# Turning one batch's queries and keys with full-width transposes, their rows sorted in the copies

## The chip, the cores and the metric

One core of one Trainium2 chip. The metric is device time in microseconds (us) of the whole kernel. A timed run lasts about 1.9 us longer than the span from first to last instruction that a profile shows. Some runs show a mean granted clock (the share of TensorE's full clock that it was given) of 0.985 to 0.995 in place of 1.000 and are longer; the ratios below count them.

## The reference

Causal attention with 16 extra "beacon" keys and values per head, then a gated feed-forward block on the result.

```python
B, H, S, Nb, D = 8, 8, 576, 16, 64
k_all = concat([beacon_k, k], axis=2); v_all = concat([beacon_v, v], axis=2)
a = softmax(where(causal, -1e9, q @ k_all.T / sqrt(D)))
x = (a @ v_all) as (4608 tokens, 512)
out = (gelu(x @ w_gate) * (x @ w_val)) @ w_out        # 512 -> 1536 -> 512
```

Before the scores of a batch can be computed, queries and keys must stand with D on the partitions: they must be turned. Batches 2 to 7 are turned by DMA. Batches 0 and 1 are turned by TensorE; three of batch 1's four head pairs are turned inside the feed-forward part of the first chunk of tokens, and it is these three turns that change.

## The kernel before

Six tokens of one head lie in a row of the loaded tile (96 rows of 6 x 64). A turn transposes 64 columns at a time, so that the two heads of a pair land on the two halves of the partitions, in a bank pair of PSUM (the memory that TensorE writes to), out of the three-buffer pool that the gate and value products also use.

```python
def tr_part(b, m, w, dst):                    # m: head pair, w: 0 queries, 1 keys
    qk, kb = qk6[b]
    for r in range(6):
        for hi in range(2):
            tr(dst[64*hi : 64*hi+64, r*96 : (r+1)*96],
               qk[0:96, w, 2*m+hi, r*D : (r+1)*D])
    if w:
        tr(dst[:, S:SK], kb[:, 2*m : 2*m+2, :])      # the beacon: 16 rows, 128 columns

def transpose_pe(b, m, by_act=False):
    t_ps = psum_s.tile([P, 2, 1024], BF16, name="t_ps", tag="s")
    for w in range(2):
        tr_part(b, m, w, t_ps[:, w, :])
    # token = 6*t + r: one sorting copy of 576 each
    # keys by VectorE, queries by ScalarE, beacon by VectorE          (cut)

for fi in range(F_TILES):                     # first chunk (b == 0), 12 gate/value pairs
    if fi >= 2:
        gate_val(b, fi, ...)                  # 8 matmuls, gelu on ScalarE, product on VectorE
    if b == 0 and fi in (6, 7, 9):
        transpose_pe(1, min(fi - 6, 2), by_act=True)
    ...                                       # (cut)
```

`psum_t` lies idle in most of the first chunk, as does `psum_o`. And GpSimd issues the loads in line with the causal masks of the attention, five of batch 2's query loads directly ahead of batch 1's first mask (`ahead(n)` issues the next n loads).

The softmax here doesn't subtract the row's maximum and nothing guards it: scores larger than these inputs give would overflow.

Of the kernel before, what the change touches and what calls it, by code (L numbers as in the profile page):

```python
# [7 lines left out]
P = 128  # L8
B, H, S, NB, D = 8, 8, 576, 16, 64
SK = S + NB  # L10
# [31 lines left out]
BF16 = mybir.dt.bfloat16  # L42
ACT = mybir.ActivationFunctionType
# [6 lines left out]
def kernel(  # L50
# [12 lines left out]
    nc = tc.nc  # L63
    keep = tc.keep_in_program_order
# [10 lines left out]
    psum_t = ctx.enter_context(tc.tile_pool(name="psum_t", bufs=1, space=bass.MemoryType.PSUM))  # L75
    psum_o = ctx.enter_context(tc.tile_pool(name="psum_o", bufs=1, space=bass.MemoryType.PSUM))
# [26 lines left out]
    qkT = qkT_sb.rearrange("p (m w c) -> p m w c", m=NPAIR, w=2)  # L103
# [9 lines left out]
    qk6 = {}  # L113
# [34 lines left out]
    def load_qk(b):  # L148
        for load in qk_loads(b):
            load()  # L150

    def load_v(b):
        for load in key_loads(v, beacon_v, v_ring[b % NRING][:, :, :, 0:D], b):
            load()
# [15 lines left out]
    def act(out_ap, in_ap, func, **kw):  # L170
        keep(nc.scalar.activation(out_ap, in_ap, func, **kw))  # L171


    def tr(out_ap, in_ap):
        n = in_ap.shape[0]
        keep(nc.tensor.transpose(out_ap, in_ap, ident[0:n, 0:n]))  # L176

    def tr_part(b, m, w, dst):
# [4 lines that stand above are left out]
                    dst[64 * hi : 64 * hi + 64, r * 96 : (r + 1) * 96],  # L183
                    qk[0:96, w, 2 * m + hi, r * D : (r + 1) * D],
                )
        if w:
            tr(dst[:, S:SK], kb[:, 2 * m : 2 * m + 2, :])
# [5 lines that stand above are left out]
        out_ap = qkT[:, m, :, NB:SK].rearrange("p w (t r) -> p w t r", r=6)  # L193
        in_ap = t_ps[:, 0:2, 0:S].rearrange("p w (r t) -> p w t r", r=6)
        keep(nc.vector.tensor_copy(out_ap[:, 1], in_ap[:, 1]))
        if by_act:
            act(out_ap[:, 0], in_ap[:, 0], ACT.Copy)
        else:
            keep(nc.vector.tensor_copy(out_ap[:, 0], in_ap[:, 0]))
        keep(nc.vector.tensor_copy(qkT[:, m, 1, 0:NB], t_ps[:, 1, S:SK]))  # L200

    def transpose_half(b, m, w, by_act=False):
        pool, tag = ((psum_o, "o"), (psum_t, "t"))[w]
        t_ps = pool.tile([P, 1024], BF16, name="t_ps", tag=tag)
        for _ in range(8 if by_act else 0):
            tr(t_ps[0:D, 640:768], idle[:, 0:D])
        tr_part(b, m, w, t_ps)
        out_ap = qkT[:, m, w, NB:SK].rearrange("p (t r) -> p t r", r=6)
        in_ap = t_ps[:, 0:S].rearrange("p (r t) -> p t r", r=6)
        if by_act:  # L210
            act(out_ap, in_ap, ACT.Copy)
        else:
            keep(nc.vector.tensor_copy(out_ap, in_ap))  # L213
        return t_ps
# [14 lines left out]
    def transpose_dma(b):  # L229
        for w, ring_w in ((0, q_ring), (1, k_ring)):  # L230
            keep(
                nc.sync.dma_start_transpose(
                    out=qkT_by_tile[:, w].rearrange("p j m c -> p (j m) c"),
                    in_=ring_w[b % NRING].rearrange("p j h d -> p (j h d)"),
                )
            )

    def scores(b, *parts):
        s_ps = psum_s.tile([P, 2, 512], FP32, name="s_ps", tag="s")
        c0 = 0  # L240
        for m, c in parts:
            score_mms(b, m, c, s_ps[:, :, c0 : c0 + CHUNK_W[c]])
            c0 += CHUNK_W[c]
        (m, c), n = parts[0], len(parts)
        o, w = CHUNK_OFF[c], CHUNK_W[c]
        act(
            exp_ring[:, m : m + n, :, o : o + w].rearrange("p g h c -> p h g c"),
            s_ps[:, :, 0 : n * w].rearrange("p h (g c) -> p h g c", g=n),
            ACT.Exp,
            scale=QK_SCALE,  # L250
        )
        if b:
            for m, c in parts:
                masks(b, m, c)
# [87 lines left out]
    def av(b, m):  # L342
        x = psum_s.tile([P, 2, 512], FP32, name="x_ps", tag="s")
        for hi in range(2):
            attend(b, m, hi, x[:, hi, :])
        normalize(b, m, x, 0, 2)

    def av_head(b, m, hi, pool, tag):
        x = pool.tile([P, 1, 512], FP32, name="x_ps", tag=tag)
        attend(b, m, hi, x[:, 0, :])  # L350
        normalize(b, m, x, hi, hi + 1)
# [10 lines left out]
    def turn_dma(b, m):  # L362
        y_sb, y_before = y_of[b * NPAIR + m], y_of.pop((b - 1) * NPAIR + m)
        keep(nc.vector.tensor_copy(y_sb[0:NB, 0, :, :], y_before[KROWS[4] - NB : KROWS[4], 4, :, :]))
        c0 = b * S - NB
        keep(
            nc.sync.dma_start_transpose(
                out=xT_sb[:, m, c0 : c0 + 5 * P].rearrange("p (j n) -> p j n", n=P),
                in_=y_sb.rearrange("p j e d -> p (j e d)"),
            )  # L370
        )
# [3 lines left out]
    def hold(b, m):  # L375
        x = xT_sb[:, m, b * S : (b + 1) * S]
        keep(nc.gpsimd.tensor_copy(hold_sb, x[:, 0 : S : S - 1]))  # L377
# [53 lines left out]
    def gate_val(ci, fi, split=False):  # L431
        gv_mms(ci, fi, *range(K_CHUNKS), split=split, last=True)
# [27 lines left out]
    def out_mms(ci, u0, u1):  # L460
        for u in range(u0, u1):
            ti, fi = divmod(u, F_TILES)
            if u == 0:
                o_of[ci] = [opool.tile([P, 4, D_MODEL], FP32, name="o_sb", tag="o_sb"), None]
            if fi == 0:
                o_of[ci][1] = out_ps(ti)
            out_mm(ci, ti, fi, o_of[ci][1])
            if fi == F_TILES - 1:
                out_store(ci, ti, o_of[ci][1])
                if ci >= N_CHUNKS - 2:  # L470
                    store(nc.sync)
# [35 lines left out]
    def ahead(n):  # L507
        for load in loads[:n]:
            load()
        del loads[:n]  # L510
# [52 lines left out]
    for b in range(B):  # L563
        u = [0]

        def o(n):
            out_mms(b - 1, u[0], u[0] + n)
            u[0] += n

        if b:  # L570
            keep(nc.scalar.preload_act_table_set(SET_EXP))
            o(3)
            scores(b, (0, 0))
            scores(b, (0, 2))
            scores(b, (0, 1))
            o(5)
            if b == 1:
                transpose_pe(1, 3)
            ahead(2)
            o(5)  # L580
            scores(b, (0, 3), (1, 3))
            scores(b, (1, 0))
            scores(b, (1, 2))
            ahead(2)
            o(5)
            av_head(b, 0, 0, psum_t, "t")
            o(1)
            scores(b, (1, 1))
            scores(b, (2, 0))
            scores(b, (2, 2))  # L590
            ahead(2)
            av_head(b, 0, 1, psum_t, "t")
            turn_dma(b, 0)
            o(7)
            scores(b, (2, 1))
            scores(b, (2, 3), (3, 3))
            scores(b, (3, 0))
            av_head(b, 1, 0, psum_o, "o")
            o(5)
            av_head(b, 1, 1, psum_o, "o")  # L600
            turn_dma(b, 1)
            scores(b, (3, 1))
            scores(b, (3, 2))
            av(b, 2)
            turn_dma(b, 2)
            o(6)
            av(b, 3)
            turn_dma(b, 3)
            o(11)
            keep(nc.scalar.preload_act_table_set(SET_GELU))  # L610
            for kk in range(K_CHUNKS):
                for fi in range(2):
                    gv_mms(b, fi, kk, last=kk == 3)
        for fi in range(F_TILES):
            if fi >= 2:
                gate_val(b, fi, fi == F_TILES - 1 and b < B - 1)
            if b == 0 and fi in (6, 7, 9):
                transpose_pe(1, min(fi - 6, 2), by_act=True)
            if fi == 0:
                if b and b + 1 < B:  # L620
                    hold(b, 3)
                    load_v(b + 1)
                if b and b + 2 < B:
                    load_qk(b + 2)
                if 2 <= b + 1 < B:
                    transpose_dma(b + 1)
                store(nc.sync)
# [40 lines left out]
```

## Time and profile before

| | before |
|---|---|
| time, median of 6 runs (366.03 in the three that the prediction had) | 365.96 us (365.76 to 366.04) |
| span in the profile | 364.4 us |
| TensorE's share of the chain that ended last | 94% |
| TensorE's time in one turn (from the single records) | 0.837 us, three times |
| between the first gate product and the first output product of chunk 0 | 24.05 us |

The page, the chain and the timeline of a turn are shown in the prediction. A chain line gives start, length and what ran. A timeline line gives start, length, engine and instruction, `xN` for N merged ones, and in brackets how long the engine was idle before it and what ended that.

### The profile page before, as it was taken

How to read it: one execution, taken by the hardware profiler on the slowest of the kernel's cores; microseconds unless marked ns; L12 is line 12 of the kernel's file. 1: busy time of each engine (PE TensorE's matmuls, PEld its weight loads, DVE VectorE, ACT ScalarE, POOL GpSimd, SP SyncE). 2: the span in 40 equal slices, each digit the busy share in tenths (PEclk: the TensorE clock that was granted, in tenths of full speed). 3: DMA queues.
4: the chain of work that ended last, by engine and by line, in shares of the span. 5: the costliest groups of instructions: out<-in, count | busy, mean ns of one | idle time of the engine just before them, and what ended most of it. 6: DMA issues, size and time to landing. Idle time of an engine off the chain costs nothing.

```text
span 364.4 us, 7627 instructions
## 1 busy us (share of the span) xinstructions
PE 354.3 (97%) x3127; PEld 184.6 (51%) x3170; DVE 155.4 (43%) x305; ACT 189.0 (52%) x243; POOL 161.2 (44%) x288
## 2 busy tenths in 40 slices
PE   7899999999999999999999999999999999999996
PEld 6664446444654456445644464446544564444443
DVE  4546545433454335343533354434444353333332
ACT  3973489136933594339723892379335953321210
POOL 8934388565537452954475554646330530000000
PEclk9999999999999999999999999999999999999999
DMA  7999999799069995999299927991697033000103
GB/s 103 175 203 204 197 124 91 125 187 186 20 121 126 199 87 65 171 216 64 57 146 208 126 35 120 178 197 24 108 142 132 17 64 114 0 0 31 58 34 112
DMA packets 160419, 41.57 MB, mean 114 GB/s; under 512 B 146944, under 2 KB 155904, under 8 KB 160384
## 3 DMA queue, kind: packets, MB, share of 16 engines
q0 software_dynamic: 104848, 19.11, 69.5%
q1 hardware_dynamic: 55536, 21.96, 29.3%
q8 instruction: 25, 0.41, 0.5%
q14 instruction: 10, 0.08, 0.1%
HBM read 38.27 MB, written 9.44 MB: 131 GB/s over the span
## 4 chain that ended last, share of the span: by engine, by line
PE 94%; issue 1%; DMA 1%; DVE 1%; POOL 1%; POOLq 0%; DVEq 0%
PE gv_ps L168 48%; PE o_ps L168 25%; PE x_ps L168 9%; PE s_ps L168 8%; PE v_ps L168 2%; PE g_ps L168 2%; DMA qk<-in_q_dram 1%; PE t_ps L176 1%; DVE qkT L213 1%; POOL qk L111 0%; PE y_ps L176 0%; DVE hT_sb L426 0%; POOL eye L480 0%; DVE o_sb L445 0%; DVE qkT L217 0%
## 5 line engine op out<-in xcount | busy, mean ns | idle before, releaser
L171 ACT ACTIVATE ge_sb<-gv_ps 128x512 bf16<-128x512 f32 x101 | 59.4, 597 | 142.8 <-PE gv_ps L168 140.6
L426 DVE TENSOR_TENSOR hT_sb<-gv_ps,ge_sb 128x512 bf16<-128x512 f32 x101 | 69.0, 691 | 113.5 <-ACT ge_sb L171 111.1
L168 PE MATMUL gv_ps<-xT_sb,wg_sb 128*128 128x512 bf16 x402 | 111.4, 379 | 0.5
L168 PE MATMUL gv_ps<-xT_sb,wv_sb 128*128 128x512 bf16 x388 | 107.9, 379 | 0.4
L171 ACT ACTIVATE expT<-s_ps 128x992 bf16<-128x992 f32 (+3 forms) x112 | 100.6, 974 | 6.5 <-PE s_ps L168 5.4
L168 PE MATMUL o_ps<-wo_sb,hT_sb 128*128 128x512 bf16 (+2 forms) x420 | 99.9, 373 | 2.0 <-issue 0.9
L298 POOL TENSOR_SCALAR_AFFINE_SELECT expT<-expT 128x256 bf16<-128x256 bf16 (+1 forms) x140 | 52.3, 390 | 52.9 <-ACT expT L171 51.8
L168 PEld LDWEIGHTS <-wv_sb 128*128 128x128 bf16 x432 | 42.3, 98 | 50.6
L168 PEld LDWEIGHTS <-wg_sb 128*128 128x128 bf16 x432 | 42.0, 98 | 50.0
L168 PEld LDWEIGHTS <-hT_sb 128*128 128x128 bf16 x444 | 39.9, 98 | 41.7 <-issue 1.7
L168 PEld LDWEIGHTS <-expT 128*128 128x128 bf16 (+1 forms) x960 | 33.6, 97 | 9.8 <-DVE y_sb L334 2.9
L445 DVE COPY o_sb<-o_ps 128x512 f32<-128x512 f32 (+2 forms) x37 | 24.9, 672 | 31.2 <-PE o_ps L168 30.2
L168 PE MATMUL x_ps<-v_sb,expT 128*128 128x65 bf16 (+1 forms) x960 | 37.4, 193 | 0.0
L111 POOL DMA_DIRECT2D v_sb<-in_v_dram x40 | 33.6, 857 | 5.9 <-DMA wv_sb<-in_moe_w_val_dram 1.7
L168 PE MATMUL s_ps<-qkT 64*128 64x80 bf16 (+5 forms) x528 | 33.1, 250 | 2.3 <-DVE qkT L217 1.3
L111 POOL DMA_DIRECT2D k_sb<-in_k_dram x30 | 25.2, 842 | 14.7 <-DMA q_sb<-in_q_dram 11.3
L334 DVE TENSOR_TENSOR y_sb<-x_ps,r_sb 128x320 bf16<-128x320 f32 (+1 forms) x47 | 28.8, 612 | 1.6
L111 POOL DMA_DIRECT2D q_sb<-in_q_dram x30 | 25.3, 874 | 5.2 <-DMA wo_sb<-in_moe_w_out_dram 3.6
L332 DVE RECIPROCAL r_sb<-x_ps 128x5 f32<-128x5 f32 (+1 forms) x47 | 9.6, 204 | 42.3 <-PE x_ps L168 42.3
L168 PEld LDWEIGHTS <-qkT 64*128 64x128 bf16 x528 | 17.1, 95 | 17.8 <-issue 12.9
L377 POOL COPY hold_sb<-xT_sb 128x2 bf16<-128x2 bf16 x6 | 1.1, 186 | 31.1 <-DMA xT_sb<-y_sb 31.1
L111 POOL DMA_DIRECT2D k_sb<-in_beacon_k_dram x6 | 3.2, 534 | 13.4 <-DMA v_sb<-in_v_dram 13.4
(54 smaller groups left out, 123.3 us busy)
## 6 DMA issues: line engine op xcount, KB each, us to landing
out_dram<-o_sb SPq DMA_DIRECT2D x35, 256.0 KB, 7.0
v_sb<-in_v_dram POOLq DMA_DIRECT2D x24, 128.0 KB, 9.1
q_sb<-in_q_dram POOLq DMA_DIRECT2D x18, 128.0 KB, 11.8
k_sb<-in_k_dram POOLq DMA_DIRECT2D x18, 128.0 KB, 5.9
wo_sb<-in_moe_w_out_dram POOLq DMA_DIRECT2D x3, 512.0 KB, 14.4
wg_sb<-in_moe_w_gate_dram POOLq DMA_DIRECT2D x2, 512.0 KB, 11.4
wv_sb<-in_moe_w_val_dram POOLq DMA_DIRECT2D x2, 512.0 KB, 13.0
v_sb<-in_v_dram POOLq DMA_DIRECT2D x8, 112.0 KB, 5.4
```

Of the source, the lines that this page charges most:

```text
L111: keep(nc.gpsimd.dma_start(out=out_ap, in_=in_ap))
L168: keep(nc.tensor.matmul(out_ap, lhsT, rhs, start=start, stop=stop, **kw))
L171: keep(nc.scalar.activation(out_ap, in_ap, func, **kw))
L176: keep(nc.tensor.transpose(out_ap, in_ap, ident[0:n, 0:n]))
L213: keep(nc.vector.tensor_copy(out_ap, in_ap))
L298: nc.gpsimd.affine_select(out=d, in_=d, pattern=[[0, 2], [1, n]], compare_op=ALU.is_ge, fill=0.0, base=0, channel_multiplier=-1,)
L332: keep(nc.vector.reciprocal(r, x[:, :, :, D:DV]))
L334: nc.vector.tensor_tensor(out=y_of[i][:, :, h0:h1, :].rearrange("p j b d -> p b j d"), in0=x[:, :, :, 0:D], in1=r.to_broadcast([P, h1 - h0 ...
L377: keep(nc.gpsimd.tensor_copy(hold_sb, x[:, 0 : S : S - 1]))
L426: nc.vector.tensor_tensor(out=h_of[ci][:, fi, :], in0=gv_of.pop((ci, fi))[1], in1=ge_sb, op=ALU.mult)
L445: keep(nc.vector.tensor_copy(o_sb[:, ti, c0:c1], o_ps))
```

## The change

Two tokens of a head (128 columns) are transposed at once: 12 transposes and the beacon in place of 24 and the beacon. The half of the partitions now holds the even or odd token, no longer the head, so four copies per operand sort rows and tokens. The turns move to the idle banks and to pairs 4, 6 and 8.

```diff
+    def transpose_wide(b, m):
+        qk, kb = qk6[b]
+        for w in (1, 0):
+            pool, tag = ((psum_o, "o"), (psum_t, "t"))[w]
+            t_ps = pool.tile([P, 1024], BF16, name="t_ps", tag=tag)
+            for hi in range(2):
+                for r in range(3):
+                    c0 = (hi * 3 + r) * 96
+                    tr(t_ps[:, c0 : c0 + 96], qk[0:96, w, 2 * m + hi, r * P : (r + 1) * P])
+            if w:
+                tr(t_ps[:, S:SK], kb[:, 2 * m : 2 * m + 2, :])
+            for hi in range(2):
+                out_ap = qkT[64 * hi : 64 * hi + 64, m, w, NB:SK].rearrange("p (t r e) -> p t r e", r=3, e=2)
+                in_ap = t_ps[:, hi * 288 : (hi + 1) * 288].rearrange("p (r t) -> p t r", r=3)
+                for e in range(2):
+                    if w:
+                        keep(nc.vector.tensor_copy(out_ap[:, :, :, e], in_ap[64 * e : 64 * e + 64]))
+                    else:
+                        act(out_ap[:, :, :, e], in_ap[64 * e : 64 * e + 64], ACT.Copy)
+            if w:
+                keep(nc.vector.tensor_copy(qkT[:, m, 1, 0:NB], t_ps[:, S:SK]))
...
-            if b == 0 and fi in (6, 7, 9):
-                transpose_pe(1, min(fi - 6, 2), by_act=True)
+            if b == 0 and fi in (4, 6, 8):
+                transpose_wide(1, (fi - 4) // 2)
```

The intent: fewer TensorE instructions and fewer changes of the array's shape, paid with more work on two engines that have time.

## The prediction

> **What bounds the kernel now.** I read the page first, for the engine that carries the span, then the chain of work that ended last, then the chain in the stretch that the change touches (30 to 48 us, the feed-forward part of the first chunk, in which batch 1's queries and keys are turned), and last the timeline of one turn.
>
> ```profile
> span 364.4 us, 7627 instructions
> PE 354.3 (97%) x3127; PEld 184.6 (51%) x3170; DVE 155.4 (43%) x305; ACT 189.0 (52%) x243; POOL 161.2 (44%) x288
> ...
> PE 94%; issue 1%; DMA 1%; DVE 1%; POOL 1%; POOLq 0%; DVEq 0%
> ```
>
> TensorE carries 94% of the chain, VectorE and ScalarE are busy about half the time. So a change pays only through what it takes from TensorE's own time; work given to VectorE and ScalarE is free as long as no matmul comes to wait for it.
>
> The chain between 30 and 48 us (start, length, what):
>
> ```profile
> 32.23 3.18 PE gv_ps L168 x14
> 35.41 0.74 PE t_ps L176 x25
> 36.15 1.83 PE gv_ps L168 x8
> 37.98 0.74 PE t_ps L176 x25
> ...
> 39.10 3.19 PE gv_ps L168 x14
> 42.28 0.74 PE t_ps L176 x25
> 43.02 1.83 PE gv_ps L168 x8
> ```
>
> Each of the three turns is on the chain with 25 transposes, and gate and value matmuls follow directly. TensorE waits here for neither a PSUM buffer nor a copy. What there is to win is inside these three pieces. One of them, in the timeline (start, length, engine):
>
> ```profile
> 34.38 1.03 PE L168 MATMUL gv_ps<-xT_sb,wv_sb 128*128 128x512 bf16 x4
> 35.13 0.88 POOL L111 DMA_DIRECT2D v_sb<-in_v_dram  x1 [1.71 <-DMA wv_sb<-in_moe_w_val_dram]
> 35.34 0.57 PEld L176 LDWEIGHTS <-qk 96*64 96x64 bf16 x24 [0.42 <-issue]
> 35.34 0.70 PE L176 MATMUL t_ps<-eye,qk 96*64 96x96 bf16 x24
> ...
> 35.97 0.09 PEld L176 LDWEIGHTS <-kb 16*128 16x128 bf16 x1
> 35.98 0.18 PE L176 MATMUL t_ps<-eye,kb 16*128 16x16 bf16 x1
> 36.08 0.69 DVE L426 TENSOR_TENSOR hT_sb<-gv_ps,ge_sb 128x512 bf16<-128x512 f32 x1 [1.03 <-ACT ge_sb L171]
> 36.08 0.55 PEld L168 LDWEIGHTS <-wg_sb 128*128 128x128 bf16 x4
> 36.09 1.04 PE L168 MATMUL gv_ps<-xT_sb,wg_sb 128*128 128x512 bf16 x4
> 36.69 0.75 DVE L195 COPY qkT<-t_ps 128x576 bf16<-128x576 bf16 x1
> ...
> 37.47 0.65 ACT L171 ACTIVATE qkT<-t_ps 128x576 bf16<-128x576 bf16 x1 [1.42 <-DVE qkT L195]
> ```
>
> The single records of the trace resolve it: the last value matmul before the turn starts at 35.032, and the next would start 216 ns later, at 35.248. The first transpose starts at 35.342, the last at 35.837, the beacon's at 35.975, the next gate matmul at 36.085. So a turn costs 36.085 - 35.248 = 0.84 us. The records also show what the count of 24 hides: the transposes start in pairs 3 to 4 ns apart, one pair every 42.5 ns, because the two heads of a pair go to opposite halves of the output partitions and run side by side.
>
> **What the Trainium skill says.** "TensorE: Matmul & The Clock Gate", section "Back-to-back issue gap", gives N / 2.4 + 2.5 ns for N moving columns: 42.5 ns for 96, which is exactly the step of a *pair* here. "TensorEngine Tiling (Array Packing)", section "Tiling Modes", says that tiles run independently and that "Changing tiling mode (not just tile) drains the TensorE". The trace agrees with both halves: the pairs overlap, and the changes of mode show as holes, 94 ns on the way in, 138 ns from the last transpose to the beacon's, 110 ns from there to the gate matmul. "ScalarE: Activation LUTs", section "What ACT_TABLE_LOAD costs", gives 186 ns + 0.833 ns an element with neighbours overlapping by some 93 ns: 666 ns for 576 elements, measured 650. "VectorE: DVE Perf Modes", section "What auto-detection actually checks", asks for step 1 on every tensor for two 16-bit elements a cycle: the sorted copy of 576 takes 749 ns, the unsorted one of the same size (xT_sb<-y_ps) 457. The new copies have steps on both sides, so I take the slow rate.
>
> **The change, part by part.** (1) *Transposes.* 24 of 64 columns become 12 of 128. It looks like half the work, but 24 in side-by-side pairs are 12 steps of 42.5 ns = 510 ns, and 12 full-width ones are again 12 steps of 42.5 ns = 510 ns. The weight loads don't set a slower step: the attention's matmuls with 128-column weights step every 29 ns. Gain from halving the count: none.
>
> (2) *Mode changes.* Before, a turn passes from full array to half-width columns, to the 16-row beacon, to the full array: three drains, and 837 - 510 = 327 ns above the steps. A 96-row, 128-column transpose should count as full-array: the turns of the attention output (128- and 80-row weights, 128 columns) pass into the gate matmuls with a step of 40 ns and no hole. Left are the two changes around the beacon, which now stands between the keys' and the queries' transposes: 138 - 42.5 = 96 ns in, about 107 ns out (the first batch's turn shows 11.442 to 11.549 from beacon to queries), and some 24 ns because the second step after a change is slower (66 instead of 42.5 ns). Sum 227 ns. Saved: 327 - 227 = 100 ns a turn, perhaps 120; three turns 0.30 to 0.37 us, all on the chain.
>
> (3) *Copies.* Per turn one VectorE copy of 576 (749 ns) and one ScalarE copy (650 ns) become four of 288 each. VectorE: 149 ns fixed + 300 = 449 ns each, 1.8 us less some overlap, with the beacon's copy of 166 ns as before. ScalarE: 186 + 240 = about 410 ns each, 1.64 us less three overlaps of some 90 = 1.35. That is 1 us more VectorE and 0.7 us more ScalarE per turn. Between two turns TensorE now spends two gate/value pairs (2 x 1.73) plus the turn, 4.2 us; VectorE has 2 x 0.69 + 1.9 = 3.3 us to do in it, ScalarE 2 x 0.60 + 1.35 = 2.55. Both fit. Latency: a gate/value buffer is reused three pairs on; its matmuls end, gelu and product take 1.3 us, and the buffer is wanted again 3.46 us after they ended. With the four copies ahead of it the next product ends about 0.8 us after that gelu could begin plus at most 0.7 us of waiting, so about 1.5 to 2 us of slack stay.
>
> (4) *Buffers.* The turn leaves the three-buffer pool of the gate/value pairs for the two banks that lie idle in the first chunk. TensorE waited for none of the three before, so this buys nothing now; it pays for the slower copies. The queries' copy no longer shares a bank with the keys' and loses its wait (1.42 us a turn behind the keys' copy), off the chain.
>
> (5) *Place.* Turns move from behind pairs 6, 7, 9 to behind pairs 4, 6, 8, so the first is wanted at about 31.8 us instead of 35.3 and the third at 40.1 instead of 42.2. The DMA records say that keys, queries and beacon for heads 0 to 3 landed at 28.18, 29.68 and 29.84, those of heads 4 to 7 at 36.36 and 37.80. Two microseconds in hand both times.
>
> Sum: -0.33 us on the chain, nothing added: 366.03 - 0.33 = 365.7.
>
> **Rivals.** *A: transposes really halve.* If full-width steps took half of 510 ns a turn, three would save 0.77 us more and the time would be 364.9. Against it: the 42.5 ns pair step equals one full-width step by the formula, and the 128-column turns of the attention output step at 56 ns, which is the same formula. *B: the copies become the bound.* If a stepped write of 2-byte elements ran at half the rate, VectorE would need 4 x 0.75 + 0.17 + 1.38 = 4.55 us per 4.2 us period, and the lag would grow over three turns to about 1 us, still inside the slack; at worst TensorE waits 0.5 us at a turn or two: 366.5. Against it: ScalarE and VectorE already run these elements at one a cycle, and the output's step is no finer than the input's. *C: the earlier place meets the loads.* A load 2 us later than recorded would stop TensorE for what is missing; the landings of one recorded run speak against it. *D: the border to batch 1 moves.* At 47.09 the last product of the chunk starts 0.45 us after all that it waits for had come, and the next scores wait some 0.2 us for it; at no other batch does that happen. I don't know its cause. If it is an accident of timing against the loads, the shift of a third of a microsecond can remove it: 365.5. It can as well make another.
>
> **Range and chances.** The centre moves a little towards D and to full-width drains cheaper than I reckon: 365.65. Repeats of one kernel differ by 0.04 us, so the range is my own doubt: down 0.45 (A in part, D), up 0.45 (B or C in small): 365.2 to 366.1. The change reaches three pieces of 0.84 us, 0.7% of the span, so over 2% faster is impossible by this mechanism; 2% slower would need 7 us of new waits, which only a broken place in the loads could make. Chances: faster 0.01, same 0.98, slower 0.01.
>
> **What would show it.** In the chain the three turns should be 13 transposes in about 0.6 us each; single records should step by 42.5 ns with no pairs, without a hole on the way in and with two around the beacon; about 0.73 us from the last gate/value step to the next. VectorE copies of 288 near 450 ns and ScalarE's near 410; no wait of TensorE for a copy or a load between 30 and 46 us. Wrong it would be if steps fell to about 25 ns (A), if copies of 288 took 0.7 us or a gate matmul waited for a product (B), or if a transpose waited for a load (C).

## The result, and the profile after

| | before | after |
|---|---|---|
| time, median of 6 | 365.96 us | 365.63 us (365.43 to 365.82) |
| ratio | | 0.9992, 95% interval 0.9979 to 1.0005 |
| span in the profile | 364.4 | 363.9 |
| one turn on TensorE | 0.837 | 0.729 |
| first gate product to first output product of chunk 0 | 24.05 | 23.66 |
| four sorting copies: VectorE, ScalarE | one of 0.75, one of 0.65 | 1.95, 1.99 |

A ratio is the mean time of one kernel's runs over that of the other's of the same rounds, so not quite the ratio of the medians quoted. Executions over 1.5% slower than the fastest of the same kernel are left out of the means.

The page of the changed kernel, its head and the chain by engine:

```profile
span 363.9 us, 7576 instructions
...
PE 353.9 (97%) x3092; PEld 184.9 (51%) x3134; DVE 158.9 (44%) x314; ACT 193.0 (53%) x252; POOL 161.1 (44%) x288
...
PE 96%; DVE 1%; issue 1%; ACT 1%; ACTq 0%
```

VectorE and ScalarE have 3.5 and 4.0 us more to do, TensorE 0.4 less. The chain in the stretch of the turns (start, length, what):

```profile
31.71 0.73 PE t_ps L176 x13
...
35.90 0.73 PE t_ps L176 x13
36.63 3.46 PE gv_ps L168 x16
40.08 0.73 PE t_ps L176 x13
```

Still three turns with gate and value products right behind them, and no copy and no load among them. (The chain's 0.73 is not the turn's cost: its pieces run from the end of one matmul to the end of another, and a matmul's end lies 0.18 to 0.38 us behind its start, by its size; so it gives 0.74 for the old turn, too little, and 0.73 where the prediction said about 0.6 for the new one. The cost is read from start to start: 31.551 to 32.280, 0.729 us.) One turn in the timeline, to hold against the one in the prediction:

```profile
31.34 0.49 PEld L176 LDWEIGHTS <-qk 96*128 96x128 bf16 x6
31.55 0.42 PE L176 MATMUL t_ps<-eye,qk 96*128 96x96 bf16 x6
...
31.90 0.18 PE L176 MATMUL t_ps<-eye,kb 16*128 16x16 bf16 x1
32.01 0.28 PEld L176 LDWEIGHTS <-qk 96*128 96x128 bf16 x6
32.02 0.43 PE L176 MATMUL t_ps<-eye,qk 96*128 96x96 bf16 x6
...
32.28 1.03 PE L168 MATMUL gv_ps<-xT_sb,wg_sb 128*128 128x512 bf16 x3
...
32.48 1.99 ACT L171 ACTIVATE qkT<-t_ps 64x288 bf16<-64x288 bf16 x4
...
32.99 1.95 DVE L218 COPY qkT<-t_ps 64x288 bf16<-64x288 bf16 x4
...
34.95 0.17 DVE L222 COPY qkT<-t_ps 128x16 bf16<-128x16 bf16 x1
```

The first weights are now loaded at 31.34, before the last value product is through, and no "0.42 <-issue" stands ahead of them: the entry into the turn has no hole. The holes around the beacon are still there (138 to 139 ns in, 111 ns out). The "x3" is a record missing from the trace, not a matmul missing from the kernel.

**Where the whole difference of the two profiles lies.** ScalarE loads a table at each border between attention and feed-forward. The starts of these loads cut every trace into the same 16 stretches, and all but a few are equal to within 0.03 us in all kernels. The differences to the kernel before, in us:

| kernel | opening, to 24 us | first chunk (the turns) | batch 1, attention and feed-forward | batch 6's attention (near 245 us) | rest | span |
|---|---|---|---|---|---|---|
| after | -0.24 | -0.41 | -0.20 | +0.28 | 0.00 | -0.57 |
| narrow_early | -0.48 | 0.00 | +0.02 | 0.00 | +0.01 | -0.45 |
| narrow_banks | -0.04 | +0.31 | -0.18 | +0.28 | +0.02 | +0.39 |
| wide_late | -0.24 | +1.92 | -0.18 | +0.28 | +0.02 | +1.80 |
| beacon_twice | -0.25 | +0.23 | -0.18 | +0.28 | +0.82 | +0.90 |
| copies_twice | -0.52 | +3.31 | -0.20 | +0.28 | +0.03 | +2.90 |
| copy_forms | -0.70 | -0.41 | -0.20 | +0.28 | +0.03 | -1.00 |
| beacon_padded | -1.12 | -0.93 | +1.30 | +0.28 | +0.06 | -0.41 |
| more_instructions | -0.97 | 0.00 | -0.20 | 0.00 | +0.02 | -1.15 |
| loads_spread | -1.17 | -0.41 | +3.43 | +0.28 | +0.02 | +2.15 |
| padded_spread | -0.78 | -0.93 | +1.82 | +0.28 | +0.05 | +0.44 |
| padded_loads_later | -0.24 | -0.93 | +4.23 | +0.28 | +0.03 | +3.37 |
| loads_later | +0.77 | -0.41 | +4.23 | +0.28 | +0.02 | +4.89 |

The opening waits for the first loads and differs by up to 1.9 us from one profiled run to the next, more than the whole effect. So spans prove nothing here: 0.24 of the 0.57 us are the opening's. The change itself is the second column, and it repeats to the hundredth (-0.41 in all four kernels that leave the first chunk as the change does). Two entries contain a lower clock, which the traces record: loads_later's opening (half clock from 11.87 to 15.28 us) and loads_spread's +3.43 (half clock from 55.36 to 58.78 us; see that run).

### The profile page after: what moved, and what is told of

The parts are those of the page before. It is cut to its first block, busy times and chain, and to the rows that moved or that the text cites. A ratio compares the mean times of both kernels' runs of the same rounds, so it can differ in the third digit from the quotient of the medians.

```text
span 363.9 us, 7576 instructions
## 1 busy us (share of the span) xinstructions
PE 353.9 (97%) x3092; PEld 184.9 (51%) x3134; DVE 158.9 (44%) x314; ACT 193.0 (53%) x252; POOL 161.1 (44%) x288
## 4 chain that ended last, share of the span: by engine, by line
PE 96%; DVE 1%; issue 1%; ACT 1%; ACTq 0%
PE gv_ps L168 48%; PE o_ps L168 25%; PE x_ps L168 9%; PE s_ps L168 8%; PE v_ps L168 2%; PE g_ps L168 2%; PE t_ps L176 2%; DVE qkT L235 1%; PE w_ps L168 1%; ACT expT L171 1%; PE y_ps L176 0%; ACT qkT L171 0%; DVE o_sb L467 0%; DVE qkT L239 0%; DVE r_sb L354 0%
## 5 line engine op out<-in xcount | busy, mean ns | idle before, releaser
L171 ACT ACTIVATE qkT<-t_ps 64x288 bf16<-64x288 bf16 (+1 forms) x13 | 6.5, 501 | 4.9 <-PE t_ps L176 4.4
```

The source lines that it names most:

```text
L171: keep(nc.scalar.activation(out_ap, in_ap, func, **kw))
```

## The experiments

All ran with correct results, except copy_forms. Times in brackets are lowest and highest.

**narrow_early**: the old turns at the new places.

```diff
-            if b == 0 and fi in (6, 7, 9):
-                transpose_pe(1, min(fi - 6, 2), by_act=True)
+            if b == 0 and fi in (4, 6, 8):
+                transpose_pe(1, (fi - 4) // 2, by_act=True)
```

> The kernel before with its three narrow turns moved to the new places (behind pairs 4, 6, 8), nothing else. My theory (the gain is mode changes of TensorE): each turn still costs 0.84 us and the time is that of the kernel before, within 0.15 us. Rival (the earlier, evenly spread places give the gain): a third of a microsecond faster than before, with less waiting somewhere between 30 and 46 us.

Measured: 365.89 us (365.87 to 366.12), ratio 1.0001 to the kernel before; turns of 0.837 us; first chunk 0.00. The places alone bring nothing.

**narrow_banks**: the changed kernel with 24 narrow transposes.

```diff
-                    tr(t_ps[:, c0 : c0 + 96], qk[0:96, w, 2 * m + hi, r * P : (r + 1) * P])
+                    for e in range(2):
+                        r0 = r * P + e * D
+                        tr(t_ps[64 * e : 64 * e + 64, c0 : c0 + 96], qk[0:96, w, 2 * m + hi, r0 : r0 + D])
```

> The changed kernel (new places, output banks, stepped copies) but with 24 narrow transposes a turn instead of 12 wide ones; the two tokens of a row go to the two halves of the output partitions. My theory: the turn costs more than the 0.73 us of the changed kernel, since two more changes of mode come back (into the narrow mode at the start, out of it at the end): about 0.88 us, so +0.15 us a turn and +0.45 us in all over the changed kernel, about 366.05. Rival (banks and copies give the gain): 0.73 us a turn and 365.6.

Measured: 366.27 us (366.01 to 366.61), ratio 1.0008; turns of 0.958 us, 0.23 more than the changed kernel's and even 0.12 more than the old ones, since the beacon in the middle gives four changes of mode and not three. The pairs step by 42.5 ns, as before. Banks and copies are not the gain; I had put this turn at 0.88, having left out the slower second step after each change (66 to 67 instead of 42.5 ns from pair to pair) and taken the last way out for cheaper than its 139 ns.

**beacon_twice**: one more beacon transpose in each turn.

```diff
-            if w:
-                tr(t_ps[:, S:SK], kb[:, 2 * m : 2 * m + 2, :])
+            tr(t_ps[:, S:SK], kb[:, 2 * m : 2 * m + 2, :])
```

> The changed kernel with the 16-row beacon transpose done a second time in each turn, behind the queries, where nobody reads it: one instruction more, but two changes of mode more. My theory: the turn grows from 0.73 us by about 0.2 us (96 ns into the 16-row mode, 110 ns out), three turns 0.6 us: about 366.2. Rival (what counts is the number of transposes and weight loads, 50 before and 26 after): it grows by 25 to 45 ns a turn, 0.1 us in all: 365.7.

Measured: 366.83 us (366.49 to 367.27), ratio 1.0026; turns of 0.934 us: one 16-row instruction costs 0.205 us. The first chunk is 0.64 us longer than the changed kernel's, as expected. The median is 0.6 us above what I expected, but two of the four runs (366.49 and 366.54) are only 0.3 above; in the profiled run, one of the other two (367.11), it is the +0.82 of "rest", where a DMA transpose of batch 6's last output landed late (4.15 us on the chain, against 2.6 at the median of these DMAs before). Whether the kernel causes this I don't know.

**beacon_padded**: the opposite, no change of mode left.

```diff
-                kpool.tile([NB, H, D], BF16, name="kb", tag="kb"),
+                kpool.tile([96, H, D], BF16, name="kb", tag="kb"),
...
+            if b:
+                nc.vector.memset(qk6[b][1], 0.0)
...
-                tr(t_ps[:, S:SK], kb[:, 2 * m : 2 * m + 2, :])
+                tr(t_ps[:, S : S + 96], kb[:, 2 * m : 2 * m + 2, :])
```

> The changed kernel with batch 1's beacon keys in a tile of 96 rows, the rows past 16 zeroed once, so that the beacon is turned by a 96-row, 128-column transpose like all others and the array never leaves its full mode in a turn. My theory: both drains around the beacon vanish, a turn takes 13 steps of 42.5 ns = 0.55 us instead of 0.73, three turns save 0.53 us: about 365.1. Rival (number of transposes counts, it stays at 13 with one of them longer): a turn stays at 0.73 us, 365.6.

Measured: 365.39 us (365.02 to 365.81), ratio 0.9988 (0.9975 to 1.0000) to the kernel before; turns of 0.554 us, where 13 steps of 42.5 ns give 0.5525; first chunk 0.52 us shorter than the changed kernel's. TensorE's part of the first turn in the timeline, without a hole:

```profile
30.68 0.42 PE L178 MATMUL t_ps<-eye,qk 96*128 96x96 bf16 x6
30.93 0.21 PE L178 MATMUL t_ps<-eye,kb 96*128 96x96 bf16 x1
30.98 0.42 PE L178 MATMUL t_ps<-eye,qk 96*128 96x96 bf16 x6
```

Together with beacon_twice this settles what a turn costs: steps of 42.5 ns plus drains, the holes at the changes of mode. Number of transposes (13, 14, 25, and 13 in the changed kernel) and cost (0.554, 0.934, 0.837, 0.729) don't go together. A wait of the beacon's weights for a load is no rival: of the changed kernel's three turns only the first has such a wait, and the hole is 138 to 139 ns in all three.

But the time did not fall by 0.53 us. The profiled run gives 1.30 back in batch 1. GpSimd's timeline there, changed kernel first, padded beacon second:

```profile
45.95 3.36 POOL L111 DMA_DIRECT2D q_sb<-in_q_dram  x4 [1.44 <-DMA wo_sb<-in_moe_w_out_dram]
49.29 1.42 POOL L320 TENSOR_SCALAR_AFFINE_SELECT expT<-expT 128x256 bf16<-128x256 bf16 x4
50.64 0.54 POOL L111 DMA_DIRECT2D k_sb<-in_beacon_k_dram  x1
51.17 0.83 POOL L111 DMA_DIRECT2D k_sb<-in_k_dram  x1
51.99 1.13 POOL L320 TENSOR_SCALAR_AFFINE_SELECT expT<-expT 128x256 bf16<-128x256 bf16 x3
```

```profile
46.31 3.37 POOL L111 DMA_DIRECT2D q_sb<-in_q_dram  x4 [1.44 <-DMA wo_sb<-in_moe_w_out_dram]
49.66 1.43 POOL L322 TENSOR_SCALAR_AFFINE_SELECT expT<-expT 128x256 bf16<-128x256 bf16 x4
51.02 0.54 POOL L111 DMA_DIRECT2D k_sb<-in_beacon_k_dram  x1
51.54 0.83 POOL L111 DMA_DIRECT2D k_sb<-in_k_dram  x1
52.37 1.48 POOL L322 TENSOR_SCALAR_AFFINE_SELECT expT<-expT 128x256 bf16<-128x256 bf16 x4
```

Both lines begin when the last output weights have landed (near 46 us) and run without a gap to the mask of the fourth key block, which the first attention needs. In the changed kernel the first of the last masks shown is done at 52.42, only 0.13 us before the matmul that needs it starts (52.555). In the other that matmul is due at 51.16 and starts at 52.85, behind a mask that is done at 52.80 (who waited for whom, in us, times, longest):

```profile
PE x_ps L170 <- POOL expT L322: 1.5, 1, 1.5
```

So past this point a faster first chunk is worth nothing as long as GpSimd's line starts at 46 us; the chain that ended last passes here through the load of these weights, 16.15 us from 29.88, and not through the turns. Of the 1.40 us by which TensorE is ahead of the changed kernel at this matmul, 0.52 are the padding's and 0.88 this run's shorter opening, so the size of the loss is that of one run.

**wide_late**: the new turns at the old places.

```diff
-            if b == 0 and fi in (4, 6, 8):
-                transpose_wide(1, (fi - 4) // 2)
+            if b == 0 and fi in (6, 7, 9):
+                transpose_wide(1, min(fi - 6, 2))
```

> The changed kernel with its wide turns at the old places (behind pairs 6, 7, 9). In the changed kernel the keys' copies end 3.57 us after a turn begins. With one pair between the first two turns, the second would begin 2.46 us after the first and find its bank still being copied: TensorE waits about 1.1 to 1.2 us, once; 366.7 to 366.8. Rival (the place is of no matter, copies are hidden anyway): 365.6.

Measured: 367.91 us (367.73 to 368.39), ratio 1.0057. The second turn and the last gate product wait for the beacon's copy, the last reader of the keys' bank:

```profile
38.62 0.28 PEld L176 LDWEIGHTS <-qk 96*128 96x128 bf16 x6 [1.49 <-DVE qkT L222]
...
46.42 0.55 PEld L168 LDWEIGHTS <-wg_sb 128*128 128x128 bf16 x4 [1.49 <-DVE qkT L222]
```

The first wait costs TensorE 1.16 us, as I had worked out. The second, also 1.16, I had overlooked: the last pair takes its gate bank from the pool that now holds the keys, two pairs after the third turn. Together 2.32 of the 2.33 us by which the first chunk is longer. The new places are no gain in themselves, but the slower copies need them.

**copies_twice**: each VectorE sorting copy done twice.

```diff
-                        keep(nc.vector.tensor_copy(out_ap[:, :, :, e], in_ap[64 * e : 64 * e + 64]))
+                        for _ in range(2):
+                            keep(nc.vector.tensor_copy(out_ap[:, :, :, e], in_ap[64 * e : 64 * e + 64]))
```

> The changed kernel with each of VectorE's four sorting copies of a turn done twice (same result): 1.95 us more VectorE work a turn. Between two turns lie 4.19 us; VectorE then has 2 x 0.69 + 3.9 + 0.17 = 5.45 us to do. The keys' bank comes free 5.5 us after a turn begins, so the second and third turn wait about 1.3 us each, 2.5 us in all: about 368. If copies were free whatever their length, as a hidden cost would be: 365.6.

Measured: 369.00 us (368.82 to 369.61), ratio 1.0088. TensorE waits 1.50 us before the second turn, 1.19 before the third and 1.01 before the last gate product: 3.70 of the 3.72 us by which the first chunk exceeds the changed kernel's. I had only the first two. Hidden work is free up to the next user of its bank: 3.57 of 4.19 us are taken in the changed kernel, 0.6 are left.

**copy_forms**: other access patterns, wrong result.

```diff
+                    if m:        # second and third turn: output dense
+                        o_ap = qkT[64 * hi : 64 * hi + 64, m, w, c0 : c0 + 288] ...
+                    if m == 2:   # third turn: input dense too
+                        i_ap = t_ps[64 * e : 64 * e + 64, hi * 288 : (hi + 1) * 288] ...
```

> Wrong result on purpose: only the access patterns of the sorting copies change. First turn as in the changed kernel; second turn with dense output (no step of two elements), third with dense output and dense input. If the step in the output makes the ScalarE copy slow (488 ns measured where I had 410), the second turn's copies fall to about 410; if it is the input's step of 96 elements, only the third's do; if it is neither (64 partitions, or the instruction itself), all stay at 488. VectorE: 478 in the first, about 450 in the second if the output's step costs, about 300 in the third, where two elements a cycle become possible.

Measured in one run (365.20 us, not used as a time). The timeline of the four copies of each turn, ScalarE and then VectorE:

```profile
32.02 1.99 ACT L171 ACTIVATE qkT<-t_ps 64x288 bf16<-64x288 bf16 x4
...
36.20 1.65 ACT L171 ACTIVATE qkT<-t_ps 64x288 bf16<-64x288 bf16 x4
...
40.38 1.65 ACT L171 ACTIVATE qkT<-t_ps 64x288 bf16<-64x288 bf16 x4
```

```profile
32.53 1.95 DVE L224 COPY qkT<-t_ps 64x288 bf16<-64x288 bf16 x4
...
36.71 1.85 DVE L224 COPY qkT<-t_ps 64x288 bf16<-64x288 bf16 x4
...
40.89 1.25 DVE L224 COPY qkT<-t_ps 64x288 bf16<-64x288 bf16 x4
```

The output's step of two elements costs ScalarE 84 ns a copy (488 to 404); the input's step costs it nothing. VectorE pays 25 ns for the output's step (478 to 453) and 150 for the input's (to 303). No two ScalarE copies overlap: they start 0.50 us apart at 488 ns each.

**more_instructions**: why do the third and fourth columns of the table differ at all? In the kernel before, the last product of the chunk starts 0.45 us after its inputs are there (rival D).

```diff
+                for j in range(3):        # after each of the old turns
+                    act(dummy[:, 2 * j : 2 * j + 2], idle[:, 0:2], ACT.Copy)
+                    keep(nc.vector.memset(dummy[:, 8 + 2 * j : 10 + 2 * j], 0.0))
```

> The kernel before with nine tiny ScalarE copies and nine tiny VectorE memsets (2 elements, nobody reads them), three of each behind each turn, as many instructions more per engine as the changed kernel has. In all wide kernels the 0.45 us hole in VectorE at the border to batch 1 was gone (that stretch 0.20 us shorter) and a hole in ScalarE came up near 245 us (that stretch 0.28 us longer), in the narrow ones neither. If the holes go by how many instructions an engine has been through, this kernel has the stretches of the wide ones: -0.20 and +0.28 us, though its turns are narrow. If they belong to the wide turns or to the timing of the loads, it has those of the kernel before: 0 and 0.

Measured in one run: 365.06 us, opening 0.97 short; turns of 0.837; batch 1 -0.20; batch 6 0.00. So the VectorE hole does go away with tiny instructions of no use, nine on each of the two engines, and does not need the wide transposes; narrow_banks, with narrow ones, had lost it too, so "in the narrow ones neither" in the expectation is wrong. An opening 0.48 us short (narrow_early) did not remove it. Which of the two engines' instructions matter was not tested, and why they do stays open. One lead, not followed up: every kernel without the hole has a transfer of 8 KB in queue q14 (instructions) between 30 and 33.1 us, which the two with the hole, the kernel before and narrow_early, do not have.

The ScalarE hole is 0.34 us long: in the changed kernel an exponential starts at 245.643, though the wait ahead of it ran at 245.303; in the kernel before the two lie 0.06 us apart (246.155 and 246.217). (The chain shows 0.63 us of "issue" at 245.77, but ScalarE is busy with that exponential until 246.507 then.) It stands in every kernel with the four copies per operand, narrow_banks too, and did not come with nine more tiny ScalarE instructions; its cause stays open.

**loads_spread, padded_spread**: four of batch 2's query loads issued between batch 1's first masks, without and with the padded beacon.

```diff
-    ahead(5)
+    ahead(1)
...
             scores(b, (0, 0))
+            ahead(1)
             scores(b, (0, 2))
+            ahead(1)
             scores(b, (0, 1))
+            ahead(1)
...
                 transpose_pe(1, 3)
+            ahead(1)
             ahead(2)
```

> The changed kernel with four of the five first loads of batch 2's queries issued between batch 1's first masks and not ahead of them (GpSimd issues loads and makes the masks in one line). In the changed kernel no attention matmul waited for a mask in this stretch, so both theories say: no difference within 0.1 us in the stretch, 365.6.

> Padded beacon and spread loads together. With the padded beacon alone the turns saved 0.53 us more, but the first attention of batch 1 waited 1.5 us for a mask that stood behind loads of batch 2's queries in GpSimd's line. If that order is what took the gain, the stretch behind the feed-forward of the first chunk loses the 1.5 us again and the time is 365.6 - 0.5 = 365.1 or less. If it is the loads themselves (the values of batch 1 land at 50 us whatever else), the wait stays under another name and the time is 365.4.

Measured: 368.62 us (367.38 to 369.08), ratio 1.0068, and 367.79 (366.66 to 369.41), ratio 1.0063. These medians mix runs at two clocks: at 1.000 one took 367.38 and three 366.66 to 366.90, at 0.991 to 0.995 three took 368.37 to 369.08 and three 368.68 to 369.41. Both expectations fell at full clock too: batch 1 takes 3.43 and 1.82 us more in the profiled runs, and of the 3.43 about 1.6 (an estimate, the difference of the two) belong to the half clock from 55.36 to 58.78 us: seven output products there take 2.99 us, in padded_spread 1.51. Six loads were still issued ahead of the mask of the fourth block, only later: GpSimd stood idle from 44.0 to 47.2 us, while the changed kernel issues four of them from 45.9 on.

**loads_later, padded_loads_later**: ten of the eleven loads behind the masks that the first attention needs.

```diff
-    ahead(5)
+    ahead(1)
...
-            ahead(2)
             o(5)
...
-            ahead(2)
+            ahead(4)
...
-            ahead(2)
+            ahead(3)
...
             scores(b, (3, 0))
+            ahead(3)
```

> Padded beacon, and ten of batch 2's eleven query and key loads issued behind the masks that the first attention of batch 1 needs (spreading them between those masks lost 2 us: GpSimd issued six of them, at 0.54 to 0.9 us each, ahead of the mask that was wanted). If GpSimd's line is what took the padded beacon's gain, the first attention starts when TensorE comes to it, the stretch behind the first chunk is 1.5 us shorter than with the padded beacon alone, and the time is about 365.0, 0.9 us under the kernel before. If the values of batch 1, which land near 50.5 us, are the next bound, the stretch gains only about 1 us of it, and the time is 365.1 to 365.3.

> The changed kernel with the same later issue of batch 2's loads. In it no matmul waited for a mask, so this alone should bring nothing where the start of the run is as in its profile (365.6), and a few tenths where the feed-forward part happens to begin earlier (365.4).

Measured: 369.58 us (369.34 to 371.02), ratio 1.0111, and 370.61 (370.35 to 371.12), ratio 1.0123 (at a clock of 1.000 alone 369.34 to 369.58 and 370.35 to 370.36). Fell again. Part of the chain of the padded one:

```profile
54.22 2.49 POOL q_sb L111 x3
56.70 1.41 POOL expT L322 x4
...
60.30 1.76 POOL expT L322 x5
62.06 2.44 POOL k_sb L111 x3
64.50 1.06 POOL expT L322 x3
```

GpSimd carries the attention of batch 1 from its first to its last mask. Eleven issues (about 9 us) and twenty masks (about 7 us) have to fit between the landing near 46 us and the last attention, and whatever is taken from the front is missing at the back. The order of the kernel before, which fills the gap ahead of the first mask, is the best of the three tried. Getting the padded beacon's half microsecond would need that line to begin earlier or to be shorter; this stays open. beacon_padded is the fastest correct variant by its median (leaving aside the single run of more_instructions), but not clear of noise against either kernel.

## Why the prediction was right

- **Transposes (1): right.** 12 full-width steps cost what 12 side-by-side pairs did; the records step by about 42 ns in both. Halving the count gave nothing. (The page gives the formula used for a single matmul on its own, and about 81 ns at 128 columns for a stream with weight loads, which the prediction left out; here the stream follows the formula: 42.5 ns at 96 columns, 56 at 128.)
- **Changes of mode (2): right, and this is the gain.** 0.73 us a turn predicted, 0.729 measured; 0.108 us saved a turn, 0.325 in three, where I had 0.30 to 0.37. beacon_twice and beacon_padded show it by adding and taking away the suspected cost alone. Inside the sum small errors cancel: the second step after the beacon is 53 ns, not 66, the hole out of it 111, not 107, and the first step of a turn 47, not 42.5. The first chunk became 0.41 us shorter; 0.02 more come from the gate product behind each turn (its successor used to start 226 ns later, now 220), and 0.045 from the step of the last value product to the first output product (261 ns before, in narrow_early and in more_instructions, 216 in every kernel with the four copies per operand, narrow_banks too); the cause of that last piece is not shown.
- **Copies (3): hidden, as said, but mis-sized.** ScalarE's four take 1.99 us, not 1.35: the step in the output costs 84 ns each and the overlap that I took off does not happen. (The sum 186 + 240 is also 426, not 410; a dense copy measured 404.) VectorE's take 1.95, near the 1.8 said. It cost nothing, because the limit was elsewhere.
- **The slack: the wrong buffer named.** I reckoned 1.5 to 2 us against the gate and value buffers. The bank of the keys is wanted again earlier; there the slack is 0.6 us, as wide_late and copies_twice show.
- **Buffers and place (4, 5): right** that they bring nothing themselves (narrow_early, narrow_banks). That the new places are needed for the new copies I had not said.
- **Rivals.** A, B and C did not occur. D did: the hole went and gave 0.20 us. What I did not see coming is a like hole in ScalarE 200 us later that took 0.28. The move of the centre towards D was therefore luck, and so is the close hit of the total: -0.41 - 0.20 + 0.28 is the -0.33 of the forecast sum, because two holes of unknown cause nearly cancel.

The measured 365.63 is 0.33 below the median before; the interval of the ratio still includes no change at all, and the repeats of the kernel before spread over 0.28 us and not the 0.04 that the prediction had seen in three. Only the trace, start to start, resolves an effect of this size.

## What to carry to other kernels

Before halving the number of small matmuls, look at the starts of single ones: where two run side by side already, as here, only the changes of the array's shape can be saved, and one odd-shaped instruction in the middle of a block costs two of them (0.2 us here). Work moved to idle engines is free only until the next user of the buffer that it reads, so find that user and its distance first. And a gain early in a kernel can be lost where a second engine's line starts at a fixed landing: look one stretch further before counting it.

## What the Trainium skill lacked or had wrong

- "TensorEngine Tiling (Array Packing)", section "Tiling Modes": says that a change of mode drains, but gives no cost. Here, start to start: 94 ns on the way from 128 columns to 64, 138 to 139 ns from the 96-row transposes into the 16-row one and, in narrow_banks, from the narrow ones to the gate product, 107 to 111 ns out of the 16-row one, and a slower second step behind (66 to 67 ns in place of 42.5 for narrow pairs, 53 for wide ones); a 16-row transpose in a full-array block 0.205 us in all.
- "ScalarE: Activation LUTs", section "What ACT_TABLE_LOAD costs": the fixed part and 0.833 ns an element give 426 ns for 288 elements; dense output took 404, output in steps of two bf16 elements 488. The page does not have the step's cost, and its overlap of neighbours was absent between these copies (starts about 500 ns apart at 488 ns each), while exponentials of the same trace overlap by 0.10 us (246.403 against an end at 246.507).
- "VectorE: DVE Perf Modes", section "What auto-detection actually checks": does not give the cost of a step in the output on top of one in the input, here 25 ns more (478 against 453 ns). What it does ask for, step 1 on every tensor, agreed (303 ns dense, 453 with a step in the input, out of PSUM).
- No page that I read has the holes in which an engine starts late although all that it waits for is there (0.45 us in VectorE, 0.34 us in ScalarE), of which the first vanished with nine more instructions on each of the two engines.
